# Attention into an expert layer on one core: q and k of three tiles over SyncE's ring, a run of ones on TensorE, attention pieces three places ahead

## The chip, the cores and the metric

The kernel runs on one core of a Trainium2 chip. Times are microseconds (us) on the device. The profile is one profiled execution of the same program, with its own time. Engines: PE is TensorE (PEld its weight loads), DVE VectorE, ACT ScalarE, POOL GpSimd, SP SyncE. A DMA is issued by an engine and then moves on that engine's ring; here SP, POOL and, once, ACT issue DMAs.

## The reference

Attention with two kinds of heads, and an expert layer on its result:

```python
# B, H, S, D = 4, 8, 768, 64; retrieval heads attend to all earlier positions,
# the others to the first n_sink = 4 and to the last window = 64
stream_keep = causal & (is_sink | in_win)
mask = where(is_retrieval, causal, stream_keep)
scores = where(mask, (q @ k.T) / sqrt(D), -1e9)
a = exp(scores - max); a = a / (sum(a) + 1e-9)
x = (a @ v).transpose(0, 2, 1, 3).reshape(3072, 512)
h = x @ w_in                 # 512 x 2048
out = (h - tanh(h)) @ w_out  # 2048 x 512
```

Inputs and output are fp32 in DRAM. The kernel computes in fp16 with fp32 sums.

## The kernel before, in words

**Tiles.** The 3072 tokens are cut into 12 tiles of 256, three to a batch. The attention of a tile is four units, one for each pair of heads (unit n = 4 x tile + pair). A unit brings its q and k to PE's layout (`st_T`: two PE transposes each for q and k, lines 843, and one copy each out of PSUM, lines 824 and 826), multiplies them (`st_S`, L941), takes exp on ACT (L961), masks, multiplies by v (L1030), divides (L1050, L1074) and transposes the result x (`st_X`, L1108). The expert layer of a tile is eight `H_unit`s, each 256 columns of w_in (L1135), tanh on ACT (L1148) and h − tanh(h) into `gt` on DVE (L1155), and then `O_mms` with w_out (L1194), whose results ACT copies out (L1170) and SP stores. O of a tile runs one tile behind its H. From the second batch on (tile 3 up) the heads are put in order of kind ("ranked"), and the transposes of q and k are made by DMA; tiles 0 to 2 use PE.

**Order.** Instructions are not written in their final order. Class `Plan` takes operations with an engine, a cost in ns and the things that they read and write, lists them on a model of the engines and of the DMA rings, and issues them in the order that comes out. The plan sets only the order on each engine; at run time every engine takes its instructions in that order and waits on semaphores. So a changed cost or due time in the plan moves instructions of many kinds.

**Loads at the start.** Tile 0's q and k come by SP, a half (four heads) at a time, in the form that the code calls `paired` (L309): two neighbouring tokens, 512 B, in one packet, so 512 packets for half the heads. v of tile 0 comes by SP in packets of 256 B (L328). fp32 data are then cast to fp16, q and k by ACT and DVE (L644, L646), v by POOL. Tiles 1 and 2 (q, k, v) come by DMAs of POOL that cast on the way (`load_cast`, 1024 packets each). The weights come by POOL too, casting: w_in in four quarters of 512 columns (L401), w_out in four pieces (L415). All of POOL's DMAs go out in one order, in which tile 1's q and k stand ahead of w_in's first quarter, and tile 2's q and k between w_out's first and second piece. From tile 3 on SP loads q, k, v, in packets of 256 B; the first of these stand behind a tiny DMA, the gate (L1308), that waits for tile 2's k.

**Masks.** A mask of 128x512 for one head is made by DVE (L523): eight for the first tile, eight more at the end of tile 1, and others for tile 2.

**Attention's place.** The pieces of a tile's attention are spread over the eight H units of the tiles before it, by `SPAN`. For ranked tiles all stand earlier by `AHEAD`, 2.0 H units (at the first ranked tile only its end does).

Of the kernel before, what the change touches and what calls it, by code (L numbers as in the profile page):

```python
# [7 lines left out]
FP32 = mybir.dt.float32  # L8
# [8 lines left out]
class Plan:  # L17
# [4 lines left out]
    ENGINES = ("PE", "ACT", "DVE", "POOL", "SP")  # L22
    OVERLAP = {"PE": 0, "ACT": 100, "DVE": 88, "POOL": 60, "SP": 0}
    PSUM = ("sc", "m", "h", "o")
    RESULT = {"PE": 200, "ACT": 0, "DVE": 0, "POOL": 0, "SP": 0}

    def __init__(self, bufs):
# [6 lines left out]
    def op(self, eng, ns, fn, r=(), w=(), dma=None, prio=None, port=False, after=None, behind=None):  # L34
        i = len(self.ops)
        deps = set() if after is None else {after}
        for k in r:
            if k in self.writer:
                deps.add(self.writer[k])
            if k[0] in self.PSUM:  # L40
# [18 lines left out]
    def run(self):  # L59
# [24 lines left out]

        def enqueue(i):
            queue[self.ops[i][0]].append(i)

        def finish(i, done):
            self.done[i] = done
            e, ns = self.ops[i][:2]  # L90
            for u in users[i]:
                to = self.ops[u][0]
                if to == e and e == "PE":
                    at = self.start[i] + ns
                else:
                    at = done + (60 if to == "PE" else 40)
                ready[u] = max(ready[u], at)
                left[u] -= 1
                if not left[u]:
                    enqueue(u)  # L100

        for i in range(n):
            if not left[i]:
                enqueue(i)
        while len(order) < n:
            t, e = min(
                [(max(free[e], min(at(i) for i in q)), e) for e, q in queue.items() if q],
                default=(1e12, None),
            )

            live = [r for r in rings.values() if r and r[0][1] <= now]
            nxt = min([r[0][1] for r in rings.values() if r and r[0][1] > now], default=1e12)
            if live:
                pk = sum(r[0][2] for r in live)
                end, r = min((now + r[0][3] * pk / r[0][2], k) for k, r in enumerate(live))
                stop = min(end, nxt, t)
                for x in live:
                    x[0][3] -= (stop - now) * x[0][2] / pk
                now = stop
                if end <= min(nxt, t):  # L120
                    i = live[r].pop(0)[0]
# [12 lines left out]
            _, ns, _, _, dma, _, port, _ = self.ops[i]  # L134
            self.start[i] = t
            order.append(i)
            free[e] = t + max(ns - self.OVERLAP[e], 40)
            if port:
                self.port = free[e]
            for u in followers[i]:  # L140
                ready[u] = max(ready[u], t + ns)
                left[u] -= 1
                if not left[u]:
                    enqueue(u)
            if dma:
                packets, each = dma
                rings["POOL" if e == "POOL" else "SP"].append(
                    [i, t + ns + (1200 if e == "POOL" else 300), each, packets * each / 16]
                )
            else:  # L150
                finish(i, t + ns + self.RESULT[e])
        self.end = max(self.done)
        for i in order:
            self.ops[i][2]()


@with_exitstack
def kernel(
# [12 lines left out]
    nc = tc.nc  # L171
# [3 lines left out]
    B, H, S, D = q.shape  # L175
# [81 lines left out]
    def program(first):  # L257
# [2 lines left out]
        op = P.op  # L260
        rot = {}

        def bank(shape, dt, tag, name):

            i = rot[tag] = rot.get(tag, -1) + 1
# [21 lines left out]

        def paired(nm, t):

            return nm != "v" and t == 0  # L290

        def load(t, names="qkv", halves=(None,), blocks=range(NB), after=None):

# [129 lines left out]

        if first:
            op(
                "ACT", 400,
                lambda: nc.scalar.dma_start(
                    out=retr_i[:], in_=is_retrieval.bitcast(I32).partition_broadcast(128)
                ),
                w=["retr"], dma=(128, 20.0),  # L430
            )
        for half in range(2):
            load(0, "qk", (half,))
            load(0, "v", (half,))
        if first:

            op("POOL", 204, lambda: nc.gpsimd.memset(ones[:], 1.0), w=["ones"])
            op(
                "ACT", 1400,
                lambda: nc.scalar.activation(out=warm[:], in_=ones[:, 0:1], func=AF.Exp),  # L440
# [70 lines left out]

            op("DVE", 165, make_rflag0, r=["sinks", "rflag"], w=["rflag0"])

        def masks(threshold, key, heads, added=False):

            for h in heads:
                how = (
                    dict(scalar2=-60000.0, op0=ALU.is_lt, op1=ALU.mult)
                    if added else dict(scalar2=None, op0=ALU.is_ge)
                )  # L520
                op(
                    "DVE", 350,
                    lambda h=h, how=how: nc.vector.tensor_scalar(  # L523
                        out=m4[:, h, :], in0=A4[:].rearrange("p a c -> p (a c)"),
                        scalar1=threshold[:, h : h + 1], **how,
                    ),
                    r=[key, "A4", "A40", "A41", "A43"], w=[("m4", h // 2)], port=True,
                )


# [346 lines left out]
                        o += 128  # L877

        first_S = {}

        def near(n):

# [217 lines left out]
        def st_X(n, tag="m", eng="DVE"):  # L1100
# [11 lines left out]
            op("PE", 112, mm, r=[("x16", n), "ident"], w=[key])  # L1112
# [147 lines left out]
        for b in range(2):  # L1260
            ones_v(b)
        cast_qk(0, (("ACT", "ACT"), ("ACT", "DVE")), (0,))
        load_cast(1, [("rv", 0, "v", 0, 1)], "qk")
        if first:
            load_w_in(*W_IN[0], ())
            load_cast(1, (), "v")
        else:
            load_cast(1, (), "v")
        for n in (0, 1):
            masks(thr, "thr", range(2 * n, 2 * n + 2), added=True)  # L1270
            st_T(n, "ACT", "DVE")
            for f in scores(n):
                f()
        cast_v(0, ("POOL", "POOL"), (0,))
        cast_qk(0, (("ACT", "ACT"), ("ACT", "DVE")), (1,))
        for n in (0, 1):
            st_A(n, 0)
            st_A(n, 1)
            masks(thr, "thr", range(2 * n + 4, 2 * n + 6), added=True)
            st_T(n + 2, "ACT", "DVE")  # L1280
            for f in scores(n + 2):
                f()
            st_X(n, "o", "ACT")
        cast_v(0, ("POOL", "POOL"), (1,))
        for n in (2, 3):
            st_A(n, 0)
            st_A(n, 1)
# [1 line left out]
        if first:  # L1289
# [2 lines left out]
            scale_v(0, "POOL")  # L1292
            load_w_in(*W_IN[3], ())
            load_w_out(0, ())
            load_cast(2, (), "q")
            load_cast(2, (), "k")
            load_w_out(1, ())
            load_cast(2, (), "v")
            load_w_out(2, ())
# [5 lines left out]
        if first:  # L1305
# [1 line left out]
            def wait_tile_2():  # L1307
                nc.sync.dma_start(out=gate[:], in_=t16[0][0:1, 0, 1, 0, 0:1])  # L1308

            gated = op("SP", 400, wait_tile_2, r=[("t16", 0, "k", 0, 0), ("t16", 0, "k", 0, 1)], w=["gate"], dma=(1, 20.0))  # L1310


        PIECES = (
# [1 line left out]
        )  # L1315
        plan = {}
        SPAN = {1: (0.0, 6.0), 2: (6.0, 16.0)}
        AHEAD = 2.0
        for t in range(3, NTT):
            lo = 16.0 + 24.0 * ((t - 3) // NG)  # L1320
            cut = (0.0, 4.5, 12.5, 24.0) if ranked(t) else (0.0, 3.4, 11.4, 24.0)
# [2 lines left out]
        for t in range(1, NTT):  # L1324
# [4 lines left out]
            for hp in range(HP):  # L1329
# [8 lines left out]
                if first and fast and (t, hp) == (2, 0):  # L1338
                    fs.append(lambda n=t * HP + hp: by_rank(first_S[n]))
                if t == 1 and hp == HP - 1:  # L1340
                    fs.append(lambda: masks(thr, "thr", range(H)))
                if first and fast and t == NG - 1 and hp == HP - 1:
                    fs.append(lambda: masks(thrr, "thrr", range(NGEN)))
                if hp == (1 if t == NG - 1 else 0) and t + 1 < NTT:
# [54 lines left out]
                O_mms(t, 0, NB * NFB)  # L1399

        with tc.manual_schedule():
            P.run()

    program(True)
    if fast:
# [37 lines left out]
```

The softmax here doesn't subtract the row's maximum and nothing guards it: scores larger than these inputs give would overflow.

## Time and profile before

| | us |
|---|---|
| median of 3 runs (lowest to highest) | 238.68 (238.62 to 239.02) |
| profiled execution | 238.46 |
| its span, first to last instruction | 236.7 |
| PE busy | 221.5 (94%) |
| ACT busy | 143.6 (61%) |
| DVE busy | 139.0 (59%) |
| POOL busy | 90.5 (38%) |
| mean TensorE clock granted | 1.00 |

Busy time is the time in which an engine has an instruction under way; matmuls are pipelined, so a busy PE need not be at its peak. "A <- B: s, n, m" in a list of waits says that A waited for B, s us in total, n times, the longest m. In a group of instructions "x2: 296/305/314" gives count and least, median and greatest duration in ns. Of a stretch of time the row has its length, then for PE, PEld, DVE, ACT and POOL the busy us with the count of instructions, then the clock that TensorE was granted, the share of the DMA engines (what their packets took, over 16 engines and the stretch; above 1 where packets overlap), and GB/s. All times are from the start of the span.

### The profile page before, as it was taken

Reading aid. Unit: us, or ns where it says so; the run is one execution under the profiler, and the core shown is the slowest. Engines: PE = TensorE matmul, PEld = TensorE weight load, DVE = VectorE, ACT = ScalarE, POOL = GpSimd, SP = SyncE. Lnnn points to the kernel's source line nnn. Section 1 sums busy time; section 2 is a strip of 40 time slices with the busy share of each in tenths; the row PEclk is TensorE's granted clock in tenths of the full one; section 3 lists DMA queues with packets and bytes.
Section 4 is the critical chain, followed back from the end, with each engine's and each line's share of the span. In section 5 each row is a group of like instructions: output and inputs, shape, how many; then the busy total and the mean of one; then the engine's idle time right before and its main releaser. Section 6 shows DMA issues by size and latency. Waiting matters only on the chain. (4 is left out here: it accounts for less than half of the span.)

```text
span 236.7 us, 5895 instructions
## 1 busy us (share of the span) xinstructions
PE 221.5 (94%) x2220; PEld 157.8 (67%) x2220; DVE 139.0 (59%) x343; ACT 143.6 (61%) x221; POOL 90.5 (38%) x218
## 2 busy tenths in 40 slices
PE   0889899999999999999999999999999999999991
PEld 0346687756776777777676777776776777777661
DVE  1856665864488657767666655667766546443300
ACT  3668677884588387466686649537759464444320
POOL 5999420089818068480814904606300000000000
PEclk9999999999999999999999999999999999999999
DMA  5999999999997999979989695998712101310121
GB/s 128 209 140 172 204 181 204 197 228 224 206 225 182 151 248 184 227 153 206 239 168 214 136 186 130 186 171 179 134 47 66 38 31 47 90 38 9 44 89 51
DMA packets 108130, 35.29 MB, mean 149 GB/s; under 512 B 100290, under 2 KB 104642, under 8 KB 108098
## 3 DMA queue, kind: packets, MB, share of 16 engines
q1 hardware_dynamic: 92642, 28.98, 60.5%
q0 software_dynamic: 15168, 5.77, 20.7%
q8 instruction: 18, 0.29, 0.5%
q10 hardware_dynamic: 288, 0.14, 0.2%
q14 instruction: 14, 0.11, 0.2%
HBM read 27.27 MB, written 6.29 MB: 142 GB/s over the span
## 5 line engine op out<-in xcount | busy, mean ns | idle before, releaser
L1135 PE MATMUL ph<-xT,win 128*128 128x256 f16 x768 | 101.7, 273 | 0.6 <-DMA win<-in_moe_w_in_dram 0.3
L1194 PE MATMUL po<-wout,gt 128*128 128x512 f16 (+1 forms) x400 | 98.0, 371 | 0.3 <-ACT ot L1170 0.3
L1148 ACT ACTIVATE th<-ph 128x512 f32<-128x512 f32 x96 | 57.6, 601 | 59.6 <-PE ph L1135 58.2
L1155 DVE SCALAR_TENSOR_TENSOR gt<-th,ph 128x512 f16<-128x512 f32 x96 | 65.4, 684 | 44.9 <-ACT th L1148 44.4
L1135 PEld LDWEIGHTS <-win 128*128 128x128 f16 x768 | 80.0, 114 | 13.0 <-issue 1.9
L961 ACT ACTIVATE pt<-sc 128x1024 f16<-128x1024 f32 (+1 forms) x78 | 68.5, 926 | 11.4 <-PE sc L941 10.9
L1194 PEld LDWEIGHTS <-gt 128*128 128x128 f16 x400 | 36.4, 98 | 24.6 <-issue 0.9
L680 POOL CAST t<-raw_rqk 128x256 f16 x72 | 28.5, 440 | 63.3 <-DMA raw_rqk<-in_k_dram 48.1
L1030 PEld LDWEIGHTS <-pt 128*128 128x128 f16 x552 | 25.9, 98 | 10.4 <-issue 0.9
L1030 PE MATMUL av<-v,pt 128*128 128x65 f16 x304 | 26.0, 195 | 0.1
L941 PE MATMUL sc<-qk 64*128 64x128 f16 (+1 forms) x412 | 23.8, 240 | 1.7 <-DVE qk L826 1.7
L941 PEld LDWEIGHTS <-qk 64*128 64x128 f16 x412 | 13.7, 94 | 13.5 <-issue 8.9
L675 POOL CAST v<-raw_rv 128x128 f16 x72 | 21.1, 335 | 4.2 <-DMA raw_rv<-in_v_dram 4.2
L1060 DVE TENSOR_TENSOR x16t<-av,rinv 128x128 f32 x72 | 20.8, 289 | 2.3 <-DVE rinv L1050 0.3
L1030 PE MATMUL av<-vf,pt 128*128 128x65 f16 x248 | 19.6, 193 | 0.0
L1170 ACT ACTIVATE ot<-po 128x512 f32<-128x512 f32 (+1 forms) x24 | 14.3, 596 | 8.5 <-PE po L1194 8.4
L996 DVE TENSOR_TENSOR pt<-pt,m 128x1024 f16<-128x1024 f16 x16 | 12.3, 768 | 8.0 <-ACT pt L961 8.0
L1050 DVE RECIPROCAL rinv<-av 128x4 f32<-128x4 f32 x48 | 8.6, 179 | 13.4 <-PE av L1030 13.4
L986 DVE TENSOR_TENSOR pt<-pt,mS 128x512 f16<-128x512 f16 x24 | 9.8, 449 | 6.7 <-ACT pt L961 6.7
L843 PEld LDWEIGHTS <-t 128*128 128x128 f16 x48 | 3.9, 107 | 8.9 <-ACT t L644 6.8
L523 DVE TENSOR_SCALAR m<-A,thr 128x512 f16<-128x512 f16 x16 | 7.4, 501 | 1.7 <-PE sc L928 1.2
L751 POOL TENSOR_TENSOR vf<-v,rflagr 128x260 f16<-128x260 f16 x12 | 7.5, 634 | 0.0
(95 smaller groups left out, 90.8 us busy)
## 6 DMA issues: line engine op xcount, KB each, us to landing
out_dram<-ot SPq DMA_DIRECT2D x23, 256.0 KB, 2.3
raw_rqk<-in_q_dram SPq DMA_DIRECT2D x20, 256.0 KB, 4.7
raw_rqk<-in_k_dram SPq DMA_DIRECT2D x20, 256.0 KB, 4.5
raw_rv<-in_v_dram SPq DMA_DIRECT2D x18, 256.0 KB, 4.4
win<-in_moe_w_in_dram POOLq DMA_DIRECT2D x4, 512.0 KB, 8.8
wout<-in_moe_w_out_dram POOLq DMA_DIRECT2D x4, 512.0 KB, 12.4
raw_rv<-in_v_dram SPq DMA_DIRECT2D x4, 128.0 KB, 4.7
t<-in_q_dram POOLq DMA_DIRECT2D x4, 128.0 KB, 9.5
```

Of the source, the lines that this page charges most:

```text
L675: nc.gpsimd.tensor_copy(out=v1s[b]()[:, lo : lo + NB, rank : rank + 1, 0:D], in_=raw_of("v", t)[:, :, at, :],)
L680: nc.gpsimd.tensor_copy(out=t16[t % 2][:, :, :, rank : rank + 1, :], in_=raws["rqk", t][0]()[:, :, :, at, :],)
L941: nc.tensor.matmul(out=sc()[:, hh, o : o + nb * 128].rearrange("p (i c) -> p i c", c=128), lhsT=ks.rearrange("p i c -> p (i c)")[p_, jb * ...
L961: lambda pt=pt, gi=gi, wid=wid, sc=sc: nc.scalar.activation(out=pt()[:, :, 512 * gi : 512 * gi + wid], in_=sc()[:, :, 0:wid], func=AF.Exp, ...
L996: nc.vector.tensor_mul(out=pv, in0=pv, in1=m4[:, h0 : h0 + 2, 256:512].unsqueeze(2).to_broadcast([128, 2, 2, 256]),)
L1030: nc.tensor.matmul(out=av()[:, i, hh, :], lhsT=pt()[:, hh, co : co + 128], rhs=vv, start=(jb == first_jb), stop=(jb == qb),)
L1060: nc.vector.tensor_mul(out=x16s[t]()[:, :, at, :], in0=av()[:, :, hh : hh + 1, 0:D], in1=rinv()[:, :, hh : hh + 1].unsqueeze(3).to_broadca ...
L1135: nc.tensor.matmul(out=ph()[:, j, :], lhsT=w()[:, cb, c0 + fb % 4 : c0 + 512 : 4], rhs=xTs[t]()[:, cb, :], start=(cb == 0), stop=(cb == HP ...
L1148: lambda: nc.scalar.activation(out=th()[:], in_=ph()[:], func=AF.Tanh, scale=1.0 / XS),
L1155: lambda: nc.vector.scalar_tensor_tensor(out=gts[t]()[:, u * FU : (u + 1) * FU, :], in0=th()[:], scalar=-XS, in1=ph()[:], op0=ALU.mult, op ...
L1170: nc.scalar.activation(out=ot()[:, c0:c1], in_=po()[:, c0:c1], func=AF.Copy, scale=1.0 / XS)
L1194: nc.tensor.matmul(out=po()[:, c0:c1], lhsT=gts[t]()[:, f, ts * 128 : ts * 128 + 128], rhs=w_out_t[f // 4]()[:, f % 4, c0:c1], start=(f == ...
```

## The change

- **Tiles 1 and 2, q and k.** `paired` holds for tiles 0 to 2. Tile 1's q and k are issued by SP right behind tile 0's loads, in halves, as fp32, and four casts on POOL make fp16 of them. Tile 2's go by SP too, behind a new tiny DMA `gate_2`, which waits for the last quarter of w_in; four casts on POOL follow. v of both tiles stays with POOL's casting DMAs. Since tokens lie in pairs, these tiles' copies out of PSUM put them in order again.
- **Gate of tile 3.** It waits for the cast of the first half of tile 2's k.
- **Weights.** The first quarter of w_in stands in the plan behind the landing of tile 0's second q half, and both casts of tile 0's v stand ahead of it on POOL.
- **Ones.** PE multiplies `ones` into an unused bank of PSUM, ten matmuls of 128x512, as soon as POOL has written `ones`. Further ones of 256 columns are put before instructions for which the plan has PE idle over 200 ns, up to the first x transpose.
- **Plan.** PE's costs count double in its first 5.6 us, the latencies of hardware DMAs are other ones, a follower becomes ready when its engine is free.
- **Masks at the end of tile 1** stand behind a result of tile 0's first H units.
- **`AHEAD`** is 3.0 in place of 2.0.

What is computed is the same. The diff, cut:

```diff
@@ Plan.run
+            if e == "PE" and t < 5600:
+                ns *= 2
...
-                ready[u] = max(ready[u], t + ns)
+                ready[u] = max(ready[u], free[e])
...
-                    [i, t + ns + (1200 if e == "POOL" else 300), each, packets * each / 16]
+                    [i, t + ns + (1200 if e == "POOL" else 1000 if t < 6000 else 400), each, packets * each / 16]
...
+        free = self.FROM
         for i in order:
+            if self.ops[i][0] == "PE":
+                idle = self.start[i] - free
+                if self.fill and idle > 200 and i != until and self.FROM < free:
+                    self.fill(int(idle * 0.5 / 107), 256)
...
@@ loads at the start
-            return nm != "v" and t == 0
+            return nm != "v" and t < 3 and (first or not t)
...
-        for half in range(2):
-            load(0, "qk", (half,))
-            load(0, "v", (half,))
+        load(0, "q", (0,))
+        load(0, "k", (0,))
+        load(0, "v", (0,))
+        load(0, "q", (1,))
+        load(0, "k", (1,))
+        load(0, "v", (1,))
...
+            wm, key = bank([128, 512], FP32, "o", "warm")
+
+            def run_up(n=10, c=512):
+                for _ in range(n):
+                    nc.tensor.matmul(
+                        out=wm()[:, 0:c].rearrange("p (a c) -> p a c", c=128), lhsT=ones[:],
+                        rhs=ones[:].unsqueeze(1).to_broadcast([128, c // 128, 128]),
+                        start=True, stop=True,
+                    )
+
+            op("PE", 2130, run_up, r=["ones"], w=[key])
+            fillers.append(run_up)
...
@@ order of the first tiles
-        load_cast(1, [("rv", 0, "v", 0, 1)], "qk")
         if first:
-            load_w_in(*W_IN[0], ())
+            load(1, "qk", (0,))
+            load(1, "qk", (1,))
+            cast_qk(1, (("POOL", "POOL"), ("POOL", "POOL")))
+        else:
+            load_cast(1, [("rv", 0, "v", 0, 1)], "qk")
+        cast_v(0, ("POOL", "POOL"), (0,))
+        cast_v(0, ("POOL", "POOL"), (1,))
+        if first:
+            load_w_in(*W_IN[0], raw_keys("q", 0, 1))
             load_cast(1, (), "v")
...
             load_w_out(0, ())
-            load_cast(2, (), "q")
-            load_cast(2, (), "k")
+            gate_2 = op(
+                "SP", 400,
+                lambda: nc.sync.dma_start(out=gate[:], in_=w_in_t[3][0]()[0:1, 0, 0:1]),
+                r=[("win", 3)], w=["gate"], dma=(1, 20.0),
+            )
+            for half in range(2):
+                load(2, "qk", (half,), after=gate_2)
+            cast_qk(2, (("POOL","POOL"),("POOL","POOL")))
             load_w_out(1, ())
             load_cast(2, (), "v")
...
-            gated = op("SP", 400, wait_tile_2, r=[("t16", 0, "k", 0, 0), ("t16", 0, "k", 0, 1)], w=["gate"], dma=(1, 20.0))
+            gated = op("SP", 400, wait_tile_2, r=t16_keys("k", 2, 0), w=["gate"], dma=(1, 20.0))
...
-        AHEAD = 2.0
+        AHEAD = 3.0
...
-                    fs.append(lambda: masks(thr, "thr", range(H)))
+                    fs.append(lambda: masks(thr, "thr", range(H), behind=[("gt",0,1)]))
...
-            P.run()
+            P.run(fillers[0] if fillers else None, first_x[0])
```

More of the change, by code (lines that the diff above doesn't have):

```diff
@@ L24 @@
     PSUM = ("sc", "m", "h", "o")
+    FROM = 5800
     RESULT = {"PE": 200, "ACT": 0, "DVE": 0, "POOL": 0, "SP": 0}
@@ L39, in op @@
                 deps.add(self.writer[k])
-            if k[0] in self.PSUM:
+            if isinstance(k, tuple) and k[0] in self.PSUM:
                 deps.update(j for j in self.readers.get(k, ()) if self.ops[j][0] != eng)
@@ L57, in op, with run @@
         return i
-    def run(self):
+    def run(self, fill=None, until=None):
+        self.fill = fill
         n = len(self.ops)
@@ L152, in run @@
         self.end = max(self.done)
+        free = self.FROM
         for i in order:
+            if self.ops[i][0] == "PE":
+                idle = self.start[i] - free
+                if self.fill and idle > 200 and i != until and self.FROM < free:
+                    self.fill(int(idle * 0.5 / 107), 256)
+                free = max(free, self.start[i] + self.ops[i][1])
+                if i == until:
+                    self.fill = None
             self.ops[i][2]()
@@ L261, in program @@
         rot = {}
+        fillers = []
         def bank(shape, dt, tag, name):
@@ L425, in program @@
             op(
-                "ACT", 400,
+                "ACT", 1150,
                 lambda: nc.scalar.dma_start(
@@ L512, in program, with masks @@
             op("DVE", 165, make_rflag0, r=["sinks", "rflag"], w=["rflag0"])
-        def masks(threshold, key, heads, added=False):
+        def masks(threshold, key, heads, added=False, eng="DVE", behind=()):
             for h in heads:
@@ L521, in masks @@
                 op(
-                    "DVE", 350,
-                    lambda h=h, how=how: nc.vector.tensor_scalar(
+                    eng, {"DVE": 350, "POOL": 560}[eng],
+                    lambda h=h, how=how: engs[eng].tensor_scalar(
                         out=m4[:, h, :], in0=A4[:].rearrange("p a c -> p (a c)"),
@@ L526, in masks @@
                     ),
-                    r=[key, "A4", "A40", "A41", "A43"], w=[("m4", h // 2)], port=True,
+                    r=[key, "A4", "A40", "A41", "A43", *behind], w=[("m4", h // 2)], port=True,
                 )
@@ L879, in program @@
         first_S = {}
+        first_x = []
         def near(n):
@@ L1110, in mm @@
                     )
-            op("PE", 112, mm, r=[("x16", n), "ident"], w=[key])
+            first_x.append(op("PE", 112, mm, r=[("x16", n), "ident"], w=[key]))
             op(
@@ L1270, in program @@
             masks(thr, "thr", range(2 * n, 2 * n + 2), added=True)
-            st_T(n, "ACT", "DVE")
+            st_T(n, *("ACT", "DVE"))
             for f in scores(n):
                 f()
-        cast_v(0, ("POOL", "POOL"), (0,))
         cast_qk(0, (("ACT", "ACT"), ("ACT", "DVE")), (1,))
@@ L1279, in program @@
             masks(thr, "thr", range(2 * n + 4, 2 * n + 6), added=True)
-            st_T(n + 2, "ACT", "DVE")
+            st_T(n + 2, *("ACT", "DVE"))
             for f in scores(n + 2):
@@ L1283, in program @@
             st_X(n, "o", "ACT")
-        cast_v(0, ("POOL", "POOL"), (1,))
         for n in (2, 3):
```

## The prediction

> **What bounds the kernel now.** I read the page's first two parts first, then the table by stretches of time, the waits of PE, single tiles, and the issues with their landings.
>
> The page: busy time by engine, and PE and DMA in 40 slices of 5.9 us.
>
> ```profile
> PE 221.5 (94%) x2220; PEld 157.8 (67%) x2220; DVE 139.0 (59%) x343; ACT 143.6 (61%) x221; POOL 90.5 (38%) x218
> ...
> PE   0889899999999999999999999999999999999991
> ...
> DMA  5999999999997999979989695998712101310121
> ```
>
> PE is full from the ninth slice on, and the DMA engines are full for the first seven. The same by stretches (length, busy us of PE, PEld, DVE, ACT, POOL, clock, DMA, GB/s):
>
> ```profile
> 6.00:10.00 4.00, 3.36 (x18) 1.45 (x18) 4.00 (x10) 2.61 (x5) 3.95 (x6) 1.00 1.52 237
> 10.00:14.95 4.95, 4.71 (x37) 2.39 (x38) 2.17 (x7) 3.34 (x7) 4.76 (x7) 1.00 1.70 132
> 14.95:18.93 3.98, 2.98 (x42) 1.75 (x41) 3.21 (x12) 2.94 (x7) 3.98 (x6) 1.00 1.51 139
> 18.93:23.70 4.77, 4.46 (x54) 3.16 (x50) 2.88 (x8) 4.06 (x7) 4.76 (x6) 1.00 1.20 191
> ...
> 60.00:80.00 20.00, 19.73 (x217) 13.82 (x216) 14.48 (x37) 13.59 (x20) 10.74 (x30) 1.00 0.95 198
> 80.00:100.00 20.00, 20.00 (x220) 15.06 (x219) 13.78 (x31) 14.49 (x21) 10.89 (x27) 1.00 1.16 213
> ```
>
> From 80 us PE has no idle time, so nothing after that can be gained except by less PE work, and the change takes none away. What can move is the start, up to about 50 us. PE's waits and, below them, two transposes of the same shape before and after 15 us:
>
> ```profile
> PE tp0q L843 <- ACT t L644: 6.0, 1, 6.0
> PE sc L941 <- DVE qk L826: 1.7, 3, 0.7
> PE xp L1108 <- DVE x L1074: 1.1, 3, 0.6
> ```
>
> ```profile
> L843 PE MATMUL tp3k<-ident,t x2: 296/305/314, 12.7 to 12.7; 128*128 128x128 f16 x2
> L843 PE MATMUL tp4q<-ident,t x2: 219/219/219, 15.2 to 15.3; 128*128 128x128 f16 x2
> ```
>
> So 6.0 us pass before the first data, then PE is named busy, but at a slow clock until about 15 us. The waits named after 6 us come to 4 us.
>
> Landings (SP's loads of tile 3 in 34 to 42 us, and the page's median for all q and k loads):
>
> ```profile
> L328 SPq DMA_DIRECT2D raw_rqk<-in_k_dram x2: 3048/4560/6073, 35.8 to 41.9; - x2
> DMA to landing us min/median/max: 6.2/10.6/11.2
> ```
>
> ```profile
> raw_rqk<-in_k_dram SPq DMA_DIRECT2D x20, 256.0 KB, 4.5
> ```
>
> SP's loads need 10.3 to 11.2 us while POOL's ring holds weights (the last of the four, issued at 41.9, 6.2), against about 4.5 elsewhere. The four w_in loads, issued at 11.13, 15.81, 16.55 and 17.28, take 5.9, 7.9, 9.8 and 11.7 us: they land at 17.0, 23.7, 26.4 and 29.0. PE's first use of w_in is at 18.93 (behind the last attention result of tile 0) and of its second quarter at 23.71, the instant it lands: the start is bound first by the chain of tile 0's attention at a slow PE, then by the weights.
>
> **The Trainium skill.** Its page "TensorE: Matmul & The Clock Gate", Part 1, says that PE runs at half clock until about 3.4 us of sustained activity; the trace agrees in kind (305 against 219 ns), though PE, 84% busy from 6 to 10 us, turned fast only near 15. Part 4 there says transposes don't count as activity; no run here shows it. "DMA: Bandwidth & Descriptors", Queues, rings and completion order, says that each DMA engine takes turns between rings, packet by packet: SP's and POOL's loads share; 10.6 against 4.5 us agrees. "SBUF — State Buffer", Who interferes with whom, says that DVE's tensor_scalar and GpSimd can lock each other out; the masks' 333 to 1155 ns fit.
>
> **The change part by part**, against the profiled execution: 238.46 us, of which span 236.7 (1.8 around it); the median of three runs is 0.2 above it.
>
> *Ones.* Ten 128x512 matmuls start when ones is written (0.90 + 0.20 = 1.1). At the slow clock one takes some 0.43 us (estimate: 512 / 1.2 GHz, the page above, Back-to-back issue gap), so they end at 5.4; the first transpose can't start before 5.95. Cost 0, with 0.55 us to spare; without that cover 0.43 us each. Four 256-column ones later stand before waits: 0 to 0.9 us, I take 0.1. Gain: PE fast from 5.5 to 8 us. The 4.71 us that PE was busy from 10 to 14.95 then shrink by up to half.
>
> *Order at the start.* DVE does eight masks at one go ahead of the copy of tp0k: they can begin at 5.25, after the flags (sinks maxima now ahead of the flags), and take 8 x 0.35 to 0.5, to 8.1 to 9.2; that copy stood at 7.46. First scores at 8.5 to 9.6, against 8.87: −0.4 to +0.7. The next units are paced by ACT (exp 0.81 + copy 0.44 = 1.25 us each) where before they came 1.37, 1.66 and 1.80 us apart: three steps save 1.1. The last transposes and x of tile 0 save some 0.5 more. First H matmul at 17.3 (16.9 to 18.2) against 18.93: gain 1.6, where w_in's first quarter has landed.
>
> *Tile 1 over SP.* Four loads of 512 packets instead of POOL's four of 1024; POOL issues four DMAs fewer (4 x 0.9) and casts four times 0.61. Their bytes are the same. w_in's first quarter goes out at about 8.1 (after the v cast) instead of 11.1, so the pause of the DMA engines near 13 us (65 GB/s in that us) is filled: 0.9 us, and v's slow stretch gives 0.3. All later weights land 1.2 us sooner (0.5 to 2.3). POOL stands before each cast: w_in's second and third quarters are queued behind tile 1's q, the fourth behind its k and second q. With k at 13 to 14 us that is free; it costs if k comes after 17. PE's use of the second quarter, just in time before, is now the limit: gain there min(1.6, 1.2) = 1.2.
>
> *Tile 2 over SP, behind w_in.* SP waits for the last w_in (29.0 − 1.2 = 27.8), issues the gate (0.74) and the loads at 28.5, 29.0 and on. Ahead of them stood nothing on SP; queued behind are tile 2 and then tile 3's gate, which now waits for POOL's cast of tile 2's k. The weights w_out, which came after tile 2's q and k, go ahead by 3.6 us. k's first half lands 4.5 us after its issue if undisturbed (33.5), 10.8 if like tile 3's (39.8). I take 6.0: like the 6.2 of the load that met only the end of POOL's ring, since these have half the packets, so half the turns. That is 35.0, cast 35.6. The instruction order puts PE's first tile-2 transposes 1.3 us of PE work later than before (there at 34.65), so PE gets there at 36.05 − 1.2 = 34.85, and waits 0.75. Gain left: 0.45. The second half of k is wanted some 11 us later: hidden.
>
> *512 B form.* The copies of tiles 1 and 2 out of PSUM take 0.44 instead of 0.28: 16 x 0.16 on DVE and ACT, 88% and below busy: 0 to 0.5, taken 0.1, in the 0.45.
>
> *Three units ahead.* Same PE work. Tile 3's first scores come 3.1 us of PE work earlier; before they were at 64.15 and their transposes landed at 60.7: slack 3.4, and tile 3 lands about 2 us sooner (one load fewer ahead of its transposes). Nothing lost, 0 to −1. Of the 0.9 us of idle that PE had from 35 to 50 (0.3 on gt, 0.6 on a DVE copy), the new order keeps about half: gain 0.45.
>
> Sum: −0.45 − 0.45 = −0.9: 237.6 profiled, **237.7** as median.
>
> **Rivals.** (1) *Tile 2 starves.* Its k lands 10.8 us after issue; cast to 40.4; PE waits 5.5 there, 4.3 more than the 1.2 won: 242.8, with some given back 242. For: the only SP loads beside weights did that. Against: that ring also held half the time's packets of v, which are short. It decides from k landing after 36.5. Slower.
> (2) *Gain and wait cancel*: k at 35.5 to 36.5; 238.2 to 239.2, 238.6.
> (3) *Tile 1 starves* behind w_in's packets: k at 17 or later, POOL holds back the fourth w_in, PE's first H past 20: 240.5. Against: tile 0's last loads, beside POOL's first, still landed in 4.6 us.
> (4) *PE doesn't speed up early* (its activity window doesn't fit the ten matmuls): only the DMA gain, nearly hidden by rival 2: 238.5.
>
> **Chances.** Forecast 0.50 (237.7; own range 236.2 to 238.2), tile 2 starves 0.28, cancel 0.10, tile 1 starves 0.07, PE slow 0.05. The range of 80%: 236.0 to 242.2 leaves out the upper part of rival 1 and a larger gain. No change (within 0.2%, 0.48 us, about what a measurement of this kernel can tell): from the forecast's upper end and rivals 2 and 4, 0.10. Faster 0.51, slower 0.39.
>
> **What would show it.** PE matmuls of 128x384 on masks near 0.35 us before 9 us; first H near 17.3; last w_in landing near 27.8; PE's wait at its first tile-2 transpose under 1 us; no wait of PE after 50 us. A wait of PE there of over 2 us, on POOL's cast, makes the prediction wrong, as do w_in landings after 29.

## The result: 242.25 us, slower by 1.4%

The changed kernel takes 242.25 us (median of 4 runs, 241.48 to 242.32), the kernel before 238.85 in the runs beside it: a ratio of 1.0138, 95% interval 1.0111 to 1.0166. The forecast was 237.7. Of the rivals, the first (tile 2 starves, 242) is what happened. The profiled execution took 242.25, its span is 240.5. Ratios and intervals, here and below, leave out runs over 1.5% above the fastest of their kernel, while medians and ranges count all runs, so a ratio isn't always the quotient of two medians.

The page of the changed kernel, busy time by engine and the slices of 6.0 us:

```profile
PE 225.0 (94%) x2234; PEld 159.3 (66%) x2234; DVE 140.5 (58%) x343; ACT 143.8 (60%) x221; POOL 88.1 (37%) x218
...
PE   7888775999999899999999999999999999999992
...
PEclk9999997999999999999999999999999999999999
...
DMA  5999997996599999997989796988410311301121
```

PE starts at once (the ones), but there is a new hole in slices 5 to 7, and the clock row, all 9 before, has a 7 in the seventh. The stretches shown of before, and in the middle the two that make the hole:

```profile
6.00:10.00 4.00, 3.32 (x34) 1.65 (x35) 2.56 (x8) 3.14 (x7) 2.51 (x3) 1.00 1.23 260
10.00:14.95 4.95, 4.08 (x62) 2.58 (x58) 3.69 (x12) 4.24 (x8) 4.95 (x8) 1.00 1.20 238
14.95:18.93 3.98, 3.95 (x48) 2.82 (x45) 1.60 (x5) 3.25 (x6) 3.98 (x7) 1.00 1.73 192
18.93:23.70 4.77, 4.03 (x53) 2.55 (x51) 4.41 (x9) 3.38 (x7) 4.40 (x7) 1.00 1.23 204
34.40:39.00 4.60, 0.01 (x1) 0.02 (x2) 0.00 (x0) 0.00 (x0) 0.61 (x1) 1.00 1.09 255
39.50:42.90 3.40, 3.40 (x20) 2.58 (x19) 1.64 (x4) 1.73 (x4) 1.54 (x3) 0.50 0.37 88
60.00:80.00 20.00, 19.95 (x226) 14.18 (x224) 13.98 (x36) 13.30 (x21) 14.13 (x36) 1.00 1.10 187
80.00:100.00 20.00, 19.32 (x221) 14.29 (x219) 12.10 (x31) 14.43 (x21) 10.09 (x29) 1.00 1.06 201
```

In the start PE gets through more instructions (144 from 6 to 18.93 us, four of them ones, against 97). Then it stands still for 4.6 us while the DMA engines are full, and works 3.4 us at half clock. From 80 to 100 us it now idles for 0.7. The waits of PE, and PE in order of time around the hole:

```profile
PE tp L872 <- POOL t L675: 4.6, 1, 4.6
PE tp7k L872 <- DVE gt L1185: 1.4, 1, 1.4
...
PE ph L1165 <- DMA xT<-x16t: 0.6, 1, 0.6
PE ph L1165 <- DMA win<-in_moe_w_in_dram: 0.6, 1, 0.6
```

```profile
31.07 1.47 PE L1165 MATMUL ph<-xT,win 128*128 128x256 f16 x12
...
33.79 0.60 PE L1165 MATMUL ph<-xT,win 128*128 128x256 f16 x4
38.99 0.40 PE L872 MATMUL tp<-ident,t 128*128 128x128 f16 x4 [4.59 <-POOL t L675]
39.22 2.48 PE L1165 MATMUL ph<-xT,win 128*128 128x256 f16 x12
```

The wait is for POOL's cast of tile 2's q. Twelve matmuls of the same form take 1.47 us before it and 2.48 behind it. The transposes whose speed was compared before are equal now, both at full clock, and SP's four loads of tile 2 land late, each over 10 us after its issue:

```profile
L872 PE MATMUL tp3k<-ident,t x2: 219/224/230, 10.8 to 10.9; 128*128 128x128 f16 x2
L872 PE MATMUL tp4q<-ident,t x2: 219/224/229, 12.2 to 12.3; 128*128 128x128 f16 x2
```

```profile
L323 SPq DMA_DIRECT2D raw_rqk<-in_k_dram x2: 491/3040/5590, 28.0 to 29.1; - x2
...
DMA to landing us min/median/max: 10.6/11.5/13.3
```

To see where time goes, one can ask of each profile when PE has done a given amount of its own work (its matmuls in order, each counted by its columns, about 0.109 us per 256, the ones left out). The table, worked out from the traces, gives that time for the kernel before, and for the others how far they are behind it (+) or ahead (−). e1 to e12 are the experiments below. Each column is one execution, and not always a typical one: those of e1 and e9 took 1.0 and 0.7 us more than the median of their runs, those of e4, e11 and e12 0.3, 1.1 and 2.4 less.

```
work  before   after     e1      e3      e4      e9     e11     e12
  0.5   8.10   -1.54   -1.37   -1.13   -1.56   -1.61   -1.57   -1.08
  6.7  19.07   -3.01   -1.88   -3.06   -3.02   -2.86   -2.46   -2.83
 11    24.07   -2.34   -0.63   -2.29   -2.36   -1.96   -2.19   -2.10
 20.3  34.65   -1.72   -0.61   -2.28   -1.74   -1.30   -2.36   -2.27
 21.7  36.12   +2.99   -0.01   -1.95   +2.74   -0.70   -1.83   -1.74
 25    39.67   +4.20   -0.45   -1.98   +2.84   -1.14   -2.10   -2.01
 45    60.03   +3.18   -1.09   -0.38   +1.81   -1.78   -3.10   -3.04
 60    74.43   +3.41   -0.75   -0.20   +2.04   -1.40   -3.12   -3.06
 70    84.52   +3.82   -0.12   +3.65   +2.59   -1.02   +0.81   -3.04
 80    93.87   +4.07   -0.10   +3.66   +2.67   -1.00   +0.83   -3.02
100   113.67   +4.01   -0.16   +3.67   +2.61   -0.44   +0.83   +1.00
218   229.13   +4.02   -0.14   +3.96   +2.63   -0.08   +0.84   +1.03
```

For the changed kernel: 3.0 us won up to the first H matmul (15.92 us, 18.93 before), 1.3 of it given back by the time that PE comes to tile 2, then 4.7 lost at tile 2's transposes and 1.2 at half clock, 1.0 won up to 63 us, and 0.8 lost from there on, 0.6 of it waiting for tile 3's x. −3.0 + 1.3 + 4.7 + 1.2 − 1.0 + 0.8 = 4.0; the spans differ by 3.8.

### The profile page after: what moved, and what is told of

Its sections match the earlier page's. It is cut to its first block, busy times and chain, and to the rows that moved or that the text cites. A ratio compares the mean times of both kernels' runs of the same rounds, so it can differ in the third digit from the quotient of the medians.

```text
span 240.5 us, 5934 instructions
## 1 busy us (share of the span) xinstructions
PE 225.0 (94%) x2234; PEld 159.3 (66%) x2234; DVE 140.5 (58%) x343; ACT 143.8 (60%) x221; POOL 88.1 (37%) x218
## 5 line engine op out<-in xcount | busy, mean ns | idle before, releaser
L1165 PEld LDWEIGHTS <-win 128*128 128x128 f16 x768 | 81.1, 114 | 14.1 <-issue 1.5
L709 POOL CAST t<-raw_rqk 128x256 f16 x72 | 27.1, 415 | 48.0 <-DMA raw_rqk<-in_k_dram 37.2
L1060 PEld LDWEIGHTS <-pt 128*128 128x128 f16 x552 | 25.1, 97 | 8.8 <-issue 0.8
L1060 PE MATMUL av<-v,pt 128*128 128x65 f16 x304 | 25.5, 193 | 0.0
L704 POOL CAST v<-raw_rv 128x128 f16 x72 | 21.6, 337 | 7.4 <-DMA raw_rv<-in_v_dram 7.4
L971 PE MATMUL sc<-qk 64*128 64x128 f16 (+1 forms) x412 | 22.9, 236 | 0.2 <-DVE qk L855 0.2
L1200 ACT ACTIVATE ot<-po 128x512 f32<-128x512 f32 (+1 forms) x24 | 14.2, 592 | 11.8 <-PE po L1224 11.4
L971 PEld LDWEIGHTS <-qk 64*128 64x128 f16 x412 | 13.6, 94 | 10.6 <-issue 7.2
L1016 DVE TENSOR_TENSOR pt<-pt,mS 128x512 f16<-128x512 f16 x24 | 10.3, 468 | 8.0 <-ACT pt L991 8.0
L1026 DVE TENSOR_TENSOR pt<-pt,m 128x1024 f16<-128x1024 f16 x16 | 11.8, 735 | 3.9 <-ACT pt L991 3.8
L675 POOL CAST t<-raw_rqk 128x512 f16<-128x512 f32 x8 | 4.9, 617 | 16.3 <-DMA raw_rqk<-in_q_dram 14.1
```

Of the source, the lines that this page charges most:

```text
L704: nc.gpsimd.tensor_copy(out=v1s[b]()[:, lo : lo + NB, rank : rank + 1, 0:D], in_=raw_of("v", t)[:, :, at, :],)
L709: nc.gpsimd.tensor_copy(out=t16[t % 2][:, :, :, rank : rank + 1, :], in_=raws["rqk", t][0]()[:, :, :, at, :],)
L971: nc.tensor.matmul(out=sc()[:, hh, o : o + nb * 128].rearrange("p (i c) -> p i c", c=128), lhsT=ks.rearrange("p i c -> p (i c)")[p_, jb * ...
L1026: nc.vector.tensor_mul(out=pv, in0=pv, in1=m4[:, h0 : h0 + 2, 256:512].unsqueeze(2).to_broadcast([128, 2, 2, 256]),)
L1060: nc.tensor.matmul(out=av()[:, i, hh, :], lhsT=pt()[:, hh, co : co + 128], rhs=vv, start=(jb == first_jb), stop=(jb == qb),)
L1165: nc.tensor.matmul(out=ph()[:, j, :], lhsT=w()[:, cb, c0 + fb % 4 : c0 + 512 : 4], rhs=xTs[t]()[:, cb, :], start=(cb == 0), stop=(cb == HP ...
```

## The experiments

"Before" beside the first four runs was 238.59, beside the next four 238.98, beside e9 to e11 238.58, beside e12 238.46. Ratios are to these, with the 95% interval.

**Tile 2 back to POOL (e1).** Theory A was rival 1; theory B that the loss lay in the other parts.

```diff
-            return nm != "v" and t < 3 and (first or not t)
+            return nm != "v" and t < 2 and (first or not t)
...
-            gate_2 = op(...)
-            for half in range(2):
-                load(2, "qk", (half,), after=gate_2)
-            cast_qk(2, (("POOL","POOL"),("POOL","POOL")))
+            load_cast(2, (), "q")
+            load_cast(2, (), "k")
```

> The changed kernel, with tile 2's q and k by POOL's casting DMAs again, in their old place between w_out's first and second piece; all else of the change stays. Theory A (tile 2 starves: SP's loads behind the last w_in share the DMA engines with w_out and v, PE waits 4.6 us for them and then runs 3.4 us at half clock): both go, 242.25 - 4.6 - about 1.2 = 236.5 us (235.8 to 237.3), PE's wait at its first tile-2 transpose under 0.5 us, no stretch of half clock after 6 us. Theory B (the loss is in the other parts: the masks on DVE that held a gt back 1.4 us, and three units ahead): not under 239.5 us.

238.01 us, 0.9978 (0.9960 to 0.9995). The wait at tile 2 is gone and with it the loss: theory B falls. It is also faster than the kernel before, but by 0.5 us, not by the 2.1 that theory A named. The runs went from 237.09 to 240.02; the profiled one, at 239.04, has a second stretch of half clock, from 16.6 to 20.0 us:

```profile
13.20:16.60 3.40, 2.02 (x30) 1.13 (x28) 2.16 (x7) 2.83 (x6) 3.40 (x5) 1.00 1.50 200
16.60:20.00 3.40, 3.01 (x14) 1.97 (x14) 0.45 (x1) 1.20 (x2) 3.40 (x6) 0.50 1.52 197
```

PE was busy for 2.02 of 3.40 us ahead of it, in pieces, the last of them followed by a wait of 1.1 us (15.9 to 17.0) for w_in's first quarter. Issued at 8.0, as in the changed kernel, this quarter landed at 16.95 instead of 15.87. Up to 18 us the two kernels have the same instructions in the same order, and so has e10, where it landed at 16.82: one execution differs from another here. So part of the expectation was wrong, and e5, e6, e9, e11 and e12 ask where the start's 3.0 us went.

**Tile 2 alone moved to SP, in the kernel before (e2).**

```diff
-            return nm != "v" and t == 0
+            return nm != "v" and t in (0, 2) and (first or not t)
...
-            load_cast(2, (), "q")
-            load_cast(2, (), "k")
+            gate_2 = op(...)
+            for half in range(2):
+                load(2, "qk", (half,), after=gate_2)
+            cast_qk(2, (("POOL","POOL"),("POOL","POOL")))
```

> The kernel before, with tile 2's q and k alone moved to SP behind the last w_in, in 512 B packets, with the gate and POOL's casts. Theory A: in the changed kernel PE's first tile-2 transpose came 12.3 us after the last w_in had landed (38.99 against 26.69); here w_in lands at 29.0, so 41.3, where PE would be at about 36.4: a wait of 4.9, some 1.5 for the clock: 244.5 us (243 to 246). Theory B: 238.7 to 240.

248.29 us, 1.0408 (1.0368 to 1.0448). The wait is the one foretold, but the half clock lasted 6.8 us (39.2 to 46.0) and further waits followed:

```profile
PE tp L843 <- POOL t L646: 5.0, 1, 5.0
PE sc L941 <- ACT pt L961: 1.7, 2, 1.1
```

Tile 2 over SP, behind w_in, is by itself enough for the loss. It costs more here, 9.7 us, than the 4.2 that e1 wins back; the profile has a longer half clock and more waits behind it.

**Hold w_out back (e3).** This takes away POOL's packets, not the gate, the form or SP's ring.

```diff
-            load_w_out(1, ())
+            load_w_out(1, t16_keys("k", 2, 0))
```

> The changed kernel, with w_out's second piece, tile 2's v and the pieces behind them on POOL held until POOL has cast the first half of tile 2's k, so that after w_out's first piece nothing of POOL's stands against SP's loads. Theory A (share of the rings): tile 2's first q lands within 5 us of its issue, at 32 to 33 instead of 38.2, PE waits under 1 us, no stretch of half clock; 237.3 us (236.3 to 238.5; a w_out piece that comes late would show as a wait of PE on w_out). Rival theory C (the lateness is the way from w_in's landing over the gate to SP's first packet, and the 512 B form, not POOL's packets): first q at 36 or later, over 240.5.

```profile
L323 SPq DMA_DIRECT2D raw_rqk<-in_q_dram x2: 385/442/500, 27.6 to 29.3; - x2
...
DMA to landing us min/median/max: 2.9/4.5/4.7
```

The same loads, issued at the same time, take 2.9 to 4.7 us instead of 10.6 to 13.3: what makes tile 2 late is POOL's queued packets, and theory C falls. But the total is 241.89, 1.0122 (1.0086 to 1.0158), not 237.3. The held weights and v now meet SP's loads of tile 3 (the second of its first two k loads landed at 50.9; 47.7 in the changed kernel). PE's lead, 2 us at 38 us, ebbs to 0.2 by 74 us; then PE waits 1.9 us for tile 3's x and works 3.4 us at half clock. The bytes were moved, not saved.

**Fill the wait (e4).**

```diff
                 def turn(x=x, tp=tp):
+                    if first and (n, x) == (8, 0):
+                        for _ in range(18):
+                            nc.tensor.matmul(out=tp()..., lhsT=ones[:], rhs=ones[:]..., start=True, stop=True)
```

> The changed kernel, with 18 matmuls of ones, 128x512, put ahead of the first tile-2 transpose, into the bank that the transposes write next: 3.9 us of work of PE within its wait of 4.6. It prices the clock alone. Theory A: the wait's end doesn't move (39.0), the stretch of half clock from 39.5 to 42.9 is gone: 1.0 to 1.6 us faster than the changed kernel, 240.6 to 241.3. If the half clock costs nothing (PE is then bound by data): 242.0 to 242.5.

241.26 us, 1.0 less than the changed kernel's 242.25 (1.0112, 1.0075 to 1.0149, against 1.0138). The clock is full throughout, and the lag behind before at work 25 is 2.84 instead of 4.20. So 4.6 us of idle cost some 0.6 (by the ratios) to 1.4 us (by the profiles) more behind them. The intervals of the two ratios overlap, so the profiles carry this:

```profile
34.40:39.00 4.60, 4.12 (x23) 1.84 (x22) 0.00 (x0) 0.00 (x0) 0.61 (x1) 1.00 1.10 254
39.50:42.90 3.40, 3.01 (x35) 2.52 (x34) 2.09 (x5) 2.15 (x6) 0.95 (x3) 1.00 0.55 130
```

**Gate 2 on the second quarter of w_in (e10).** Would packets of 1 KB on the other ring be kinder than 4 KB?

```diff
-                lambda: nc.sync.dma_start(out=gate[:], in_=w_in_t[3][0]()[0:1, 0, 0:1]),
-                r=[("win", 3)], w=["gate"], dma=(1, 20.0),
+                lambda: nc.sync.dma_start(out=gate[:], in_=w_in_t[1][0]()[0:1, 0, 0:1]),
+                r=[("win", 1)], w=["gate"], dma=(1, 20.0),
```

> The changed kernel, with gate 2 on w_in's second quarter instead of the fourth: SP's loads of tile 2 are issued at about 22.4 us, not 27.6, and share with w_in's packets of 1 KB, not w_out's of 4 KB. The plan puts PE's first tile-2 transposes 4 us of PE work earlier. Theory A (what a shared load costs is set by the other ring's packet[...]): q lands 6 to 8.5 us after its issue, not 10.6; w_in's last quarter comes 1 to 3 us later; PE waits 0 to 2 us at tile 2; 238 to 240 us, 2 to 4 faster than the changed kernel. Theory C (any load behind a gate while POOL's ring is full takes 10 to 11 us): q at 33, PE waits 3 and more, 241 to 243.

242.05 us, 1.0148 (1.0093 to 1.0204), and q took 10.7 us again: by the load and the total theory C came true, though PE's wait at tile 2 was 1.4 us, not 3 and more. The packets say why, and it isn't theory C's reason. q was issued at 22.55, its first packet went at 26.07, and by then w_in's packets were nearly through. The packets of each ring from 26 to 30 us (nearly all in w_out's time), and from 31 to 34 (v's 128 B packets), count, MB and share:

```profile
q0 software_dynamic: 211, 0.74, 91.6%
q1 hardware_dynamic: 209, 0.11, 12.8%
```

```profile
q1 hardware_dynamic: 953, 0.47, 78.8%
q0 software_dynamic: 965, 0.14, 64.7%
```

One packet of SP's for one of POOL's, beside 4 KB packets and beside 128 B ones. The Trainium skill, "DMA: Bandwidth & Descriptors", Queues, rings and completion order, says that the DMA engines take turns between rings packet by packet; here are the counts. Beside w_out SP gets 209 packets in 4 us, beside v 953 in 3, and nearly alone (the changed kernel, 38 to 39 us, 10 of POOL's) 588 in 1. Whether w_in's 1 KB packets would be kinder to tile 2 stayed untested, since the loads came too late to meet them. But in the changed kernel's start, from 12 to 14 us, tile 1's loads did meet them:

```profile
q0 software_dynamic: 329, 0.34, 99.6%
q1 hardware_dynamic: 197, 0.09, 23.5%
```

That is about 100 packets of SP's per us, twice as many as beside w_out, and fewer than one for one; why fewer isn't shown.

**Where the start's lead goes.** First, three units ahead: two instead of three in e1 (e5), and three alone in the kernel before (e8).

```diff
-        AHEAD = 3.0
+        AHEAD = 2.0
```

> The kernel of the first experiment (the change, with tile 2 by POOL) with the attention of the ranked tiles two H units ahead again, as before. PE's order up to 45 us is the same. Theory D (three units ahead costs: it lets SP's transposes of tile 3's x meet SP's loads, 5.1 us from issue to landing against 2.3 before, and the lead of 0.75 us that the first experiment had at 74 us is gone at 80): 0.5 to 0.9 faster than the first experiment, 237.3 us. Theory E (three units ahead gains or is hidden): 238.0 to 238.7.

> The kernel before, with three units ahead alone; PE's order differs from about 45 us on. Theory D: SP's transposes of tile 3's x come late, PE waits for them near 76 to 80 us, 0.3 to 0.9 slower: 239.0 to 239.5. Theory E: 238.2 to 238.7.

e5: 238.45 us, 0.9978 (0.9955 to 1.0001), the ratio of e1. e8: 238.79, 0.9965 (0.9941 to 0.9989), though by the medians it is 0.2 us from before, whose own runs there spread from 237.6 to 243.5; in its profile the lag behind before is 0.22 us at 27 us and 0.28 at the end. Theory D falls: three units ahead costs nothing. That it gains is not shown. In e5, too, tile 3's x was long on its way (issued at 74.1 and 75.3, landed at 78.6 and 79.1).

Next, the ones: left out of e1 (e6), and added alone to the kernel before (e7, the ten with their bank, without the fillers).

```diff
-            op("PE", 2130, run_up, r=["ones"], w=[key])
-            fillers.append(run_up)
```

> The kernel of the first experiment without the ones and their fillers; the order of all other instructions is the same. Theory F (the ones make PE fast from about 6 us and so give most of the 3.0 us of lead at the first H matmul): the stretch of full clock begins at 12 to 17 us, the first H matmul falls back from about 16 to 17.5 or later; but w_in's second quarter lands at 21.7 all the same, so of this only 0.3 to 0.8 reaches the end: 238.3 to 238.8. Theory G (the weights alone set the start): 238.0, equal; or faster, if PE's half-clock stretch at 16.6 in the first experiment comes from the early start.

> The kernel before, with the ten matmuls of ones alone. Theory F: full clock from 5 to 8 us, the first H matmul at 17.1 to 17.6 instead of 18.9 (w_in's first quarter lands at 17.05). Theory H (w_in's second quarter, landed at 23.67 and used at once before, is the limit behind it): PE waits 1 to 2 us for it and the end moves by less than 0.4: 238.3 to 238.7. If the chain of attention alone were the limit: 237.2.

e6: 239.27 us, 1.0010 (0.9988 to 1.0032); full clock from 15.9 us, first H at 18.21 us, 0.7 ahead of before. With the ones it came at 15.9 in the changed kernel, e3 and e4, and at 16.7 to 17.0 in e1, e5 and e10, where w_in's first quarter landed that late. So the ones are worth some 1.2 to 2.3 us at the first H (theory F in kind; its 238.3 to 238.8 was too low), and at the end at most the 0.3% between 0.9978 and 1.0010, whose intervals overlap. e7 was a surprise: 244.51 us, 1.0148 (1.0049 to 1.0247). What the profile shows is another order on DVE. With the ones in the plan it got tp0k's copy ahead of the first four masks, stood still for 1.9 us, and the other four masks then fell beside POOL's multiplies and DMA issues:

```profile
7.21 0.45 DVE L837 COPY qk<-tp0k 128x256 f16<-128x256 f16 x1 [1.90 <-PE tp0k L854]
...
10.50 4.77 DVE L534 TENSOR_SCALAR m<-A,thr 128x512 f16<-128x512 f16 x4
```

1.19 us for one mask, and PE waited 2.9 us (12.2 to 15.1) for it. PE's clock had fallen already at 9.2, before that wait, after a stretch of 3.4 us in which PE was busy for 1.4, and it came back at 19.4. Whether ones alone pay in the kernel before is left open.

Then the clock itself: ten more ones in e1's waits (e9). `keep(o, n)` multiplies ones n times into the bank that is written next.

```diff
                 def turn(x=x, tp=tp):
+                    if first and (n, x) in ((4, 1), (7, 1)):
+                        keep(tp()..., 3)
...
                     w, c0 = w_in_t[fb // 4]
+                    if first and (t, u, j) in ((0, 0, 0), (0, 2, 0)):
+                        keep(ph()..., 2)
```

> The kernel of the first experiment with ten more matmuls of ones, 128x512, in four places where its PE waits (three before the second k transposes of tile 1's first pair and of its last, two before the first use of w_in's first and of its second quarter), 2.2 us of PE work, for the most part within waits of 0.6 to 1.4 us. It tests whether the first experiment fell short of its 236.5 by the half clock from 16.6 to 20.0 us. Theory K (it did: the stretch cost 1.2 to 2.4 us of lead, in a share of the runs): no stretch of half clock after 7 us, 237.2 us (236.7 to 237.8), and a narrower spread than 237.1 to 240.0. Theory L (the lead is eaten by w_in's second quarter and DVE in any case, so the clock there is free): 238.0 to 238.8, the ones' own time added.

238.47 us, 0.9988 (0.9973 to 1.0002); runs from 237.78 to 239.47. The half clock is gone (full from 3.9 us to the end), the spread is narrower, and the lead is 1.4 us at 74 us instead of 0.75. But at the end it is 0.08: the clock isn't the whole answer, and theory K's number was missed. The lead was 1.0 us up to 110 us; it went in two waits for transposes of q and k, 0.5 us at 110.8 and 0.3 at 125.6:

```profile
PE sc L981 <- DMA qk<-t: 0.8, 2, 0.5
```

So theory L's number holds, but not its reason.

Then the masks, which stretch beside POOL in the changed kernel as well: eight at one go in 2.19 us while POOL waits, three in 3.08 while POOL multiplies.

```profile
5.11 2.19 DVE L552 TENSOR_SCALAR m<-A,thr 128x512 f16<-128x512 f16 x8
...
21.55 3.08 DVE L552 TENSOR_SCALAR m<-A,thr 128x512 f16<-128x512 f16 x3
```

In e11 those at the end of tile 1 are not held behind a gt.

```diff
-                    fs.append(lambda: masks(thr, "thr", range(H), behind=[("gt",0,1)]))
+                    fs.append(lambda: masks(thr, "thr", range(H)))
```

> The kernel of the first experiment, with the eight masks at the end of tile 1 no longer held behind a result of tile 0; the plan puts four of them elsewhere on DVE, and moves some 30 instructions of PE's. Theory M (masks of DVE stretch to 1.0 us beside POOL's multiplies, and held as they are they put a gt of H back, for which PE waits 0.6 to 1.4 us at 25 us): the wait of PE on gt goes, 0.3 to 0.6 faster than the first experiment, 237.5. Rival N: the masks stretch wherever they stand near POOL's work, and the next thing behind them on DVE is late instead: 238.0 or more.

241.57 us, 1.0078 (1.0045 to 1.0110), runs from 238.47 to 243.75. In its profile (240.43) PE is 3.1 us ahead of before from 48 to 71 us, and at work 20.3, where the changed kernel has 1.7 of its lead left, it has 2.4: 0.7 more, which the masks can have given, though the plan also moved some 30 of PE's instructions and issued w_in's fourth quarter at 13.3 instead of 16.7. Then it loses all at once:

```profile
PE ph L1165 <- DMA xT<-x16t: 2.1, 1, 2.1
```

Tile 3's x landed at 78.7 us, and 3.4 us at half clock follow. So a loss came, but at a place that neither theory M nor rival N named. In the kernel before the same x landed at 77.5 and PE used it at 78.75: it had 1.2 us to spare. In e1, e5, e9 and e11 its first transpose was issued at 73.7, 74.1, 73.6 and 72.8 (before: 73.9), and the x landed at 79.4, 79.1, 78.4 and 78.7. PE's lead did not bring its landing forward, and as long as that is so, a lead of much more than 1.2 us can't pass it. The two transposes take 2.3 us each in the kernel before and 3.2 to 5.5 in e11, behind SP's loads. The last run (e12) plans tile 6's loads behind them, in e11's kernel.

```diff
                             after=gated if first and t == 1 else first_S[t * HP + hp],
+                            r=[("xT", t - 1, "all", 1)] if ranked(t - 1) and t == NG + 1 else (),
```

> The kernel of e11_tile2_pool_masks, in which SP's loads of tile 6 are planned behind its transposes of tile 3's x, not ahead of them. In e11 PE was 3.1 us ahead of the kernel before from 36 to 71 us, and lost it all between 71 and 85: it waited 2.1 us for tile 3's x (transposes issued at 72.8 and 75.5, landed at 78.2 and 78.7, behind loads; before 73.9 and 75.2, landed at 76.2 and 77.5 and used at 78.75), then ran 3.4 us at half clock. Theory P (the start's gain is capped by tile 3's x, which comes late behind SP's own loads): its transposes land within 3 us of their issue, PE waits under 0.4 us there, no half clock at 80, 2 us or more of the lead stays: 236.3 us (235.7 to 237.3). Rival Q (the supply of data as a whole is the cap: SP's loads that come later make tile 6 late): the wait turns up at tile 4's x or tile 6's scores instead, 238 to 240.

242.84 us, 1.0186 (1.0146 to 1.0225). The profiled execution, at 240.48, is the fastest of the six; what the others lost beyond it no trace shows. In it the x's transposes, issued at 70.9 and 72.1, landed within 3.9 and 3.1 us. The wait on tile 3's x is gone and the lead of 3.0 us holds to 91 us, as theory P has it; then comes what rival Q named, at tile 6's own transposes:

```profile
PE sc L971 <- DMA qk<-t: 2.4, 1, 2.4
```

and 3.4 us at half clock, from 99.1 to 102.5. The total is above the 238 to 240 of rival Q as well. Here the transfer that was put ahead on SP's ring came in time, and the one that was put behind it came late. Whether another order of SP's loads could carry the lead to the end was not tried.

## Why the prediction was wrong

**The step that failed** is in "Tile 2 over SP": "I take 6.0: like the 6.2 of the load that met only the end of POOL's ring". The first q took 10.6 us and the first k 11.4, as rival 1 had it with 10.8, and PE waited 4.6 us instead of 0.75. The 6.2 belonged to a load issued at 41.94, when POOL's ring had 2.4 us of work left (its last landing is at 44.4); the three loads that took 10.3 to 11.2 were issued from 34.8 on, and landed at 45.1 to 47.1, just behind the same landing. So those times are better read as the rest of POOL's queue than as a price per packet. In the changed kernel, at 27.6, POOL's ring had three pieces of w_out, the end of another and two v loads left, until 42 us, and this could be read beforehand from the order of POOL's queue: moving tile 2 behind w_in put those bytes beside it. "Half the packets, so half the turns" does not help as long as that queue lasts: of the four loads' 2048 packets SP got 555 from 31 to 37 us, beside 1027 of POOL's, and then 492 in the one us from 37 to 38, when POOL's had fallen to 20. The rival's mechanism held. That its number, 242, held too is partly luck: it had 5.5 us for the wait (4.6) and nothing for the clock behind it.

**Left out altogether:** the half clock behind such a wait, priced at 0.6 to 1.4 us by e4. The page "TensorE: Matmul & The Clock Gate", in its section on HAM oscillation, names idle gaps of over 3.4 us; the trace agrees with 4.59 us of idle and 3.4 at half clock. But half clock came with shorter waits as well: 1.7 (e7), 1.9 (e3, e10), 2.1 (e11) and 2.4 us (e12), and in e1 one of 1.1. Waits of 1.4 us (the changed kernel at 25 us, e10 at 34) kept the full clock. Where the limit lies these traces don't say.

**The start:** ones, cost right (ten in 4.40 us, ended 5.56, first transpose 5.94), gain too small: first H at 15.92, not 17.3. Part of this is the masks, 0.27 us each with POOL waiting where 0.35 to 0.5 were taken: first scores came at 7.74 (8.28 in e6, without ones), not 8.5 to 9.6. The ones' 1.2 to 2.3 us at the first H had no term of their own in the 1.6. "Tile 1 over SP" was right in kind, and short: w_in's quarters landed 1.2, 2.1, 2.3 and 2.3 us sooner (1.2 was taken). The second k half landed only at 16.6, with no loss: the fourth quarter, issued at 16.7, stood on POOL behind two multiplies (14.1 to 16.2) and a cast, not behind that load. PE came to tile 2 at 34.4 (34.85 foretold).

**The masks:** the hold behind gt was not costed; it made PE wait 1.4 us at 25 us.

**512 B form:** the copies took 0.45 us, hidden. **Three units ahead:** 0.45 was taken as gain; e5 and e8 show neither gain nor loss.

**What can move is the start:** right, but not enough. PE's zero idle from 80 us said nothing of how closely the data arrived: tile 3's x with 1.2 us to spare, tile 5's at 109.88 for a use at 110.05. The start gained more than forecast, and without tile 2's wait (e1) the end moved by 0.5 us. So the forecast's −0.9 would hardly have come even with k in time; in e3, where k was in time, the total was 241.89. (A slip of the sum: 238.68 − 0.9 is 237.8, not 237.7.)

## What to carry to other kernels

A load put beside another ring's queue of large packets is priced by what is left in that ring, not by its own length; list what is still queued there at the time of issue. A wait of PE costs clock as well: in these traces every one of 1.7 us or more that began at full clock brought half clock with it. Before counting on a lead, look for the next transfer that PE uses, and how long before its use it lands: a busy PE hides slack of 0.2 us as well as of 5.

## What the runs showed of the hardware, unexpected

- SP's first packet of a load went 3.5 to 3.75 us after its issue when POOL's ring was full (27.56 to 31.26 in the changed kernel; before, e2 and e10 alike), and 1.05 us after it when that ring had run dry (e3).
- Stretches of one clock are multiples of 3.41 us (10.2, 34.1, 75.1; half clock 3.4, 6.8, 10.2), and they start at another place in each execution: the same instructions of the start fell to half clock in e1, where w_in's first quarter landed 1.1 us later, and not in the changed kernel.
- A mask of 128x512 on DVE took 0.27 us while POOL waited and 1.03 to 1.19 beside POOL's multiplies and DMA issues. The page "SBUF — State Buffer", Who interferes with whom, tells of the lock; its size was not expected.
